# Weight decode, v rows, key low parts, mixed tokens and the transfer plan of an attention and channel-mix kernel

## The chip, the cores and the metric

The kernel runs on one core of a Trainium2 chip. A core has five engines that run their own instruction queues and wait for each other through semaphores: TensorE (PE in the profile), VectorE (DVE), ScalarE (ACT), GpSimd (POOL) and SyncE (SP). Here SP issues every DMA. The metric is device time in microseconds, lower is better. A measured time is the median of several executions, and a profile is of one execution.

## The reference

The program is an attention layer whose output feeds a channel mix with a gate:

```python
# q, k, v: (8, 8, 1152, 64)
q_pool = q.reshape(B, H, S // 2, 2, D).mean(axis=3)        # 576 pooled queries
scores = scale * np.matmul(q_pool, k.transpose(0, 1, 3, 2))
scores = scores - np.max(scores, axis=-1, keepdims=True)
attn = np.exp(scores)
attn = attn / (np.sum(attn, axis=-1, keepdims=True) + 1e-09)
out = np.matmul(attn, v)                                   # (8, 8, 576, 64) -> x: (8, 576, 512)
x_prev = np.concatenate([zeros, x[:, :-1, :]], axis=1)
xk = mu_k * x + (1.0 - mu_k) * x_prev
xr = mu_r * x + (1.0 - mu_r) * x_prev
k = np.maximum(xk @ w_k, 0.0)                              # w_k: 512 x 1024
v = k * k @ w_v                                            # w_v: 1024 x 512
r = 1.0 / (1.0 + np.exp(-(xr @ w_r)))                      # w_r: 512 x 512
return r * v
```

There are 64 heads (8 batches of 8), and 4,608 mixed tokens of 512 features.

## The kernel before, in words

**Precision.** All products run on 16-bit operands, with each fp32 operand split into a high and a low part; three products (high by high, high by low, low by high) then stand for one.

**Attention.** A head has 1,152 keys in 9 chunks of 128, and 576 queries in 6 blocks of 96. `prep` loads a head's k and v, casts k to fp16 (L397, ScalarE), subtracts for the low part (L399, VectorE), and transposes both by DMA in two pieces of 5 and 4 chunks (L404). v gets a high part (L412), a low part (L415) and a scaled copy `vb` (L418). The tile `vt` has rows of 130 fp16 elements per key chunk, `vb` rows of 66. `queries` does the same for the pooled queries of two heads. `block` multiplies a block's scores into one of three PSUM tiles `s` (L445), takes their maximum on VectorE (L452, L458) with two small matmuls (L455, L460), writes the negative maximum into the low query operand (L463), adds the low products (L469), and takes the exponential (L475). GpSimd makes the low part of the exponentials (L477). `window` multiplies 128 queries' exponentials with v: nine chunks of three matmuls (L495 and L497 from `vt`, L502 from `vb`) into the PSUM bank `a`; a head has five windows, all in that bank. The bank is then divided by the row sums (L517 to L520), and after every second head it is transposed (L532) and copied to the token tile `xt` (L535).

**Channel mix.** Tokens go in 18 tiles of 256. `mix` blends each token with the one before it, feature chunk by feature chunk: L604 on ScalarE, L607 on VectorE into the fp32 tile `xk` or `xr`. The matmul's high operand is the upper half of each fp32 word, read in place as bf16 with a step of two elements (`top`); L612 on VectorE subtracts it for the low part `xlk` or `xlr`. `ff` does, per tile, 96 products for `w_k` with 256 moving columns, and per 128 tokens 12 products for `w_r` and 24 for `w_v` with 512 moving columns, all on L632. The relu, the square and the gate run on ScalarE, VectorE and GpSimd.

**Weights.** The three weight tensors arrive as words in which `weights` finds a value in two pieces. They come in 20 chunks of 128 by 512, each loaded by L553 and rebuilt once: L564 on ScalarE writes to the PSUM bank `f`; L566, L567 and L569 on VectorE shift it and join sign and low bits; L571 casts to the high part and L572 on GpSimd subtracts for the low part. The bank `f` also holds the channel mix's products.

**Order.** Nothing is issued as the loops are written. Each piece of work is handed to a planner (`Issue`) with a duration, the buffers it reads and writes, and a key. The planner plays the whole program forward and backward twelve times against its own table of durations and latencies, keeps the shortest order that it finds, and the instructions are then issued in that order on each engine, DMAs too.

The first channel-mix tile needs all 8 heads of batch 0 and all of `w_k`. From then on PE has channel-mix products to put between the attention's blocks.

Of the kernel before, what the change touches and what calls it, by code (L numbers as in the profile page):

```python
# [3 lines left out]

# [42 lines left out]
LATE, SLACK = 0.08, 0.1  # L47


class Issue:  # L50

    LAT = {("DMA", "*"): 2.0, ("*", "DMA"): 1.22, ("PE", "DMA"): 1.46, ("PE", "PE"): 0.0,
           ("PE", "ACT"): 0.26, ("PE", "DVE"): 0.2, ("DVE", "PE"): 0.17, ("ACT", "PE"): 0.17,
           ("ACT", "POOL"): 0.18, ("DVE", "POOL"): 0.155, ("POOL", "PE"): 0.11, ("ACT", "DVE"): 0.142,
           ("DVE", "ACT"): 0.128, ("DVE", "DVE"): 0.12, ("ACT", "ACT"): 0.13, ("POOL", "POOL"): 0.13}  # L60

# [3 lines left out]
    def lat(self, a, b):  # L65
        for k in ((a, b), (a, "*"), ("*", b)):
            if k in self.LAT:
                return self.LAT[k]
        return 0.18

    def add(self, eng, dur, fn, r=(), w=(), key=0.0, port=None, tail=2.0):
# [23 lines left out]
        self.ops.append((eng, dur, fn, key, deps, eng == "POOL" if port is None else port, tail))  # L95

    @staticmethod
    def play(eng, dur, pred, succ, prio, wait, port):
# [3 lines left out]
        left = [len(p) for p in pred]
        ready = [0.0] * N
        start = [0.0] * N
        free, pend, avail = {}, {}, {}
        way = 0.0
        for n in range(N):
            e = eng[n]
            if e not in free:
                free[e], pend[e], avail[e] = 0.0, [], []  # L110
            if not left[n]:
                heapq.heappush(pend[e], (0.0, n))
        push, pop = heapq.heappush, heapq.heappop
        for _ in range(N):
# [17 lines left out]
            key, n = pop(av)  # L132
            if port[n] and way > t:

# [6 lines left out]
                else:  # L141
                    soon = [(rt, prio[m], m) for rt, m in pe if not port[m] and rt < way]
                    if soon:
                        rt, k2, m = min(soon)
                        push(av, (key, n))
                        pe.remove((rt, m))
                        heapq.heapify(pe)
# [620 lines left out]
```

## Time and profile before

| | us |
|---|---|
| median of 3 runs (1186.74 to 1193.13) | 1187.83 |
| span of the profiled execution, first to last instruction | 1190.5 |
| PE, DVE, ACT, POOL busy in the span | 1127.0, 933.5, 839.2, 527.8 |
| PE without a matmul in flight in the first 170 us | 55.1 |
| the same in all that follows | 8.4 |

The span is the profiled execution's own time as far as the profile gives it; nothing else is listed for that execution. It lies 2.7 us above the median of the timed runs and inside their range. A matmul's busy time in the profile is its time in flight (about 194 ns for 65 columns), and many are in flight at once, so PE's busy share tells when it has nothing to do, and the steps between the starts of its matmuls tell how fast it goes.

### The profile page before, as it was taken

Reading aid. Unit: us, or ns where it says so; the run is one execution under the profiler, and the core shown is the slowest. Engines: PE = TensorE matmul, PEld = TensorE weight load, DVE = VectorE, ACT = ScalarE, POOL = GpSimd, SP = SyncE. Lnnn points to the kernel's source line nnn. Section 1 sums busy time; section 2 is a strip of 40 time slices with the busy share of each in tenths; the row PEclk is TensorE's granted clock in tenths of the full one; section 3 lists DMA queues with packets and bytes.
Section 4 is the critical chain, followed back from the end, with each engine's and each line's share of the span. In section 5 each row is a group of like instructions: output and inputs, shape, how many; then the busy total and the mean of one; then the engine's idle time right before and its main releaser. Section 6 shows DMA issues by size and latency. Waiting matters only on the chain.

```text
span 1190.5 us, 45818 instructions
## 1 busy us (share of the span) xinstructions
PE 1127.0 (95%) x19504; PEld 933.0 (78%) x19504; DVE 933.5 (78%) x1827; ACT 839.2 (70%) x1674; POOL 527.8 (44%) x549
## 2 busy tenths in 40 slices
PE   3868689999999999999999999999999999999998
PEld 3757687888879787888888787979787888888565
DVE  5879898888798888888888878888887888774431
ACT  4767767777877777777878687776877777765543
POOL 2546455454545444544545354545354444533111
PEclk9989889999999999999999999999999999999999
DMA  8777754656555553545455544544455444210000
GB/s 199 176 164 167 174 113 112 131 122 136 101 110 138 125 115 74 114 119 110 100 117 116 120 104 102 115 95 110 107 113 110 100 86 100 51 35 2 28 18 27
DMA packets 226412, 126.71 MB, mean 106 GB/s; under 512 B 161696, under 2 KB 198560, under 8 KB 226208
## 3 DMA queue, kind: packets, MB, share of 16 engines
q1 hardware_dynamic: 226208, 123.79, 46.8%
q8 instruction: 152, 2.49, 0.9%
q14 instruction: 52, 0.43, 0.1%
HBM read 67.11 MB, written 9.44 MB: 64 GB/s over the span
## 4 chain that ended last, share of the span: by engine, by line
PE 85%; DVE 5%; ACT 4%; DMA 3%; issue 2%; SPq 0%; POOL 0%; ACTq 0%; DVEq 0%
PE f L632 33%; PE s L445 11%; PE s L469 11%; PE a L502 7%; PE a L495 7%; PE a L497 7%; PE s L632 4%; DVE mx L452 2%; ACT pf L475 2%; PE s L455 2%; PE a L632 2%; PE s L460 1%; PE a L532 1%; DMA qT<-qn 1%; DMA vr<-in_v_dram 1%
## 5 line engine op out<-in xcount | busy, mean ns | idle before, releaser
L477 POOL TENSOR_SCALAR pl<-pf 128x864 f16<-128x864 uint16 x384 | 379.1, 987 | 445.3 <-ACT pf L475 429.1
L452 DVE TENSOR_REDUCE mx<-s 128x96 f16<-128x864 f32 x384 | 402.8, 1053 | 83.5 <-PE s L445 47.2
L475 ACT ACTIVATE pf<-s 128x864 int32<-128x864 f32 x384 | 337.5, 890 | 103.2 <-PE s L469 81.6
L445 PE MATMUL s<-qT,ks 128*128 128x96 f16 x3456 | 222.4, 208 | 29.2 <-ACT pf L475 14.7
L497 PE MATMUL a<-vt,pf 128*128 128x64 f16 x2880 | 233.9, 194 | 0.0
L495 PE MATMUL a<-vt,pf 128*128 128x65 f16 x2880 | 233.5, 194 | 0.0
L469 PE MATMUL s<-qT,ks 128*128 128x96 f16 x3456 | 218.8, 209 | 14.6 <-ACT qT L463 11.3
L445 PEld LDWEIGHTS <-ks 128*128 128x128 f16 x3456 | 186.1, 99 | 52.6 <-issue 23.8
L469 PEld LDWEIGHTS <-ks 128*128 128x128 f16 x3456 | 184.3, 99 | 35.3 <-issue 13.5
L495 PEld LDWEIGHTS <-pf 128*128 128x128 f16 x2880 | 202.0, 99 | 6.7
L497 PEld LDWEIGHTS <-pf 128*128 128x128 f16 x2880 | 193.1, 98 | 8.2
L463 ACT ACTIVATE qT<-s 1x96 f16<-1x96 f32 x384 | 92.5, 243 | 104.3 <-PE s L460 94.1
L458 DVE TENSOR_REDUCE mb<-s 96x1 f16<-96x128 f32 x384 | 109.0, 285 | 71.5 <-PE s L455 65.0
L502 PE MATMUL a<-vb,pl 128*128 128x65 f16 x2880 | 153.9, 194 | 3.4 <-POOL pl L477 3.4
L632 PE MATMUL f<-xk,wk_lo 128*128 128x256 bf16 x496 | 136.9, 276 | 0.0
L632 PE MATMUL f<-xk,wk_hi 128*128 128x256 bf16 x496 | 136.8, 276 | 0.1
L632 PE MATMUL f<-xlk,wk_hi 128*128 128x256 f16 x496 | 134.4, 271 | 0.1
L502 PEld LDWEIGHTS <-pl 128*128 128x128 f16 x2880 | 122.8, 99 | 8.0 <-POOL pl L477 3.8
L663 POOL TENSOR_TENSOR gl<-g 128x512 f16<-128x512 f32 x72 | 78.5, 1091 | 104.6 <-ACT g L661 102.7
L632 PEld LDWEIGHTS <-wk_hi 128*128 128x128 f16 x1152 | 104.6, 97 | 13.0 <-issue 0.2
L632 PE MATMUL f<-wv_hi,g 128*128 128x512 f16 x240 | 90.9, 379 | 1.1 <-ACT em L682 1.1
L632 PE MATMUL f<-wv_hi,gl 128*128 128x512 f16 x240 | 90.9, 379 | 0.0
(90 smaller groups left out, 1895.0 us busy)
## 6 DMA issues: line engine op xcount, KB each, us to landing
kr<-in_k_dram SPq DMA_DIRECT2D x64, 288.0 KB, 3.2
vr<-in_v_dram SPq DMA_DIRECT2D x64, 288.0 KB, 3.3
qr<-in_q_dram SPq DMA_DIRECT2D x32, 320.0 KB, 3.7
ks<-ks SPq DMA_DIRECT2D x64, 144.0 KB, 3.1
out_dram<-em SPq DMA_DIRECT2D x36, 256.0 KB, 2.2
qr<-in_q_dram SPq DMA_DIRECT2D x32, 256.0 KB, 3.4
st<-in_moe_w_k_dram SPq DMA_DIRECT2D x8, 512.0 KB, 4.8
st<-in_moe_w_v_dram SPq DMA_DIRECT2D x8, 512.0 KB, 4.3
```

Of the source, the lines that this page charges most:

```text
L445: nc.tensor.matmul(cols(c, c + 1), ks1[hp][:, c, :], qhi, start=(c == c0), stop=False, skip_group_check=True)
L452: op("DVE", 0.967, lambda: nc.vector.tensor_reduce(mxz, grid(0, NC).rearrange("p c q -> p q c"), axis=AX.X, op=ALU.max), r=[("s", z)], w=[ ...
L458: op("DVE", 0.199, lambda: nc.vector.tensor_reduce(mbz[0:QN], s[0:QN, 0:P], axis=AX.X, op=ALU.max), r=[("s", z)], w=[("mb", z)], key=t + O ...
L463: op("ACT", 0.133, lambda: nc.scalar.activation(qlo[QN:QN + 1], s[QN:QN + 1, 0:QN], AF.Prelu, scale=1.0 - EPS, alpha=(1.0 + EPS) / (1.0 - ...
L469: nc.tensor.matmul(cols(c, c + 1), ks2[hp][:, c, :], qlo, start=False, stop=True, skip_group_check=True)
L475: op("ACT", NC * QN / 1200 + 0.051, lambda: nc.scalar.activation(pf[:, :, rows], grid(0, NC), AF.Exp, bias=SHIFT, scale=0.125 / (2.0 * SQ) ...
L477: op("POOL", NC * QN / 1000 + 0.066, lambda: nc.gpsimd.tensor_scalar(pl[:, :, rows], half(pf, U16, 0)[:, :, rows], LO, 1.0, op0=ALU.mult, ...
L495: nc.tensor.matmul(a_b[:, a0:a0 + VN], half(pf, F16, 1)[:, c, rows], vt[jv][:, c, D:D + VN], start=(w == 0 and c == 0), stop=False, skip_g ...
L497: nc.tensor.matmul(a_b[:, a0:a0 + D], half(pf, F16, 1)[:, c, rows], vt[jv][:, c, 0:D], start=False, stop=False, skip_group_check=True)
L502: nc.tensor.matmul(a_b[:, a0:a0 + VN], pl[:, c, rows], vb[jv][:, c, 0:VN], start=False, stop=(c == NC - 1), skip_group_check=True)
L632: nc.tensor.matmul(ps, terms[i][0], terms[i][1], start=(first and i == 0), stop=(i == last), skip_group_check=True)
L663: op("POOL", 2 * n * 0.0018 + 0.1, lambda f2=f2: nc.gpsimd.tensor_tensor(gl[:, f2, 0:n], g32[:, f2, 0:n], gh[:, f2, 0:n], op=ALU.subtract) ...
```

## The change

- The weights' low bits are converted by ScalarE (L587 of the changed kernel, into the buffer `em`), and the word is rebuilt in the SBUF buffer `ex` rather than in the PSUM bank `f`. VectorE has two steps per chunk (L590, L598) where it had three. Variants `"A"` and `"P"` of the code are not used (`DEC_K`, `DEC_RV` are `"D"`).
- Rows of `vt` have 136 elements and rows of `vb` 72, so each starts at a multiple of 16 bytes. The columns that are read are the same.
- For the first 8 heads GpSimd subtracts the key's low part instead of VectorE (`KN_POOL`), and windows of every second of these heads go to the bank `f` instead of `a` (`ALT`).
- A mixed token chunk is cast by ScalarE (L641) to its own contiguous fp16 tile `xh`, and this is the matmul operand in place of the strided upper halves. The fp32 chunk lies in one of three small buffers `xm`.
- A head's keys, and two heads' queries from the second pair on, are transposed by one DMA instead of two.
- The planner treats the DMAs as one line: a DMA has an issue time and a load, transfers land in order, and SP runs at most 8 us ahead of the line. The forward plan starts from keys with noise of a fixed seed. Several durations in its table are other numbers. A tile's two halves (`"k"` and `"r"`) are handed over by two calls of `ff`.

```diff
+KN_POOL, VT_POOL, XL_POOL = 8, 0, 0
+DEC_K, DEC_RV = "D", "D"
+ALT = 1
+QSPLIT = 1
+WDEP = [("ks1", 1), ("ks2", 0), ("vr", 1)]
+AHEAD2 = 0
+SEED, SPREAD = 2, 1.0
...
+    ISSUED, LANDED, AHEAD = 1.44, 0.52, 8.0
...
+            if e == "DMA" and ahead:
+                line = max(t + self.ISSUED, line) + load[n]
+                free[e] = max(end, line - self.AHEAD)
+                land = line + self.LANDED
+            elif e == "DMA":
+                free[e] = land = t + max(dur[n], load[n])
...
+        rnd = random.Random(SEED)
+        start, _ = self.play(p, succ, pred, [o[3] + rnd.gauss(0.0, SPREAD) for o in ops], wait, True)
...
-    vt = bufs("vt", NV, [P, NC, 2 * D + 2], F16)
-    vb = bufs("vb", NV, [P, NC, D + 2], F16)
+    vt = bufs("vt", NV, [P, NC, 2 * D + 8], F16)
+    vb = bufs("vb", NV, [P, NC, D + 8], F16)
...
-    xm = {n: const.tile([P, NG, T], F32, name=f"x{n}") for n in "kr"}
-    xl = {n: const.tile([P, NG, T], F16, name=f"xl{n}") for n in "kr"}
+    xm = bufs("xm", 3, [P, T], F32)
+    xl = {n: bufs(f"xl{n}", 1, [P, NG, T], F16) for n in "kr"}
+    xh = {n: bufs(f"xh{n}", 1, [P, NG, T], F16) for n in "kr"}
...
+        for j0, j1 in JS if n < QSPLIT else ((0, NQ),):
...
-            op("DVE", nn / 960 + 0.069, lambda cs=cs: nc.vector.tensor_tensor(
+            e, en, d = ("POOL", nc.gpsimd, nn * 0.0022 + 0.1) if n < KN_POOL else ("DVE", nc.vector, nn / 960 + 0.069)
+            op(e, d, lambda cs=cs, en=en: en.tensor_tensor(
                 kn[i][:, cs, D:P], kr[i][:, cs], kn[i][:, cs, 0:D], op=ALU.subtract),
                r=[("kr", i), ("kn", i, c0)], w=[("knl", i, c0)], key=key + 1, port=True)
-        for c0, c1 in ((0, 5), (5, NC)):
-            cs = slice(c0, c1)
-            op("DMA", 0.14 * (c1 - c0) + 0.08, lambda cs=cs: nc.sync.dma_start_transpose(
-                ks1[i][:, cs], kn[i][:, cs].rearrange("p c x -> p (c x)")),
-               r=[("kn", i, c0), ("knl", i, c0)], w=[("ks1", i, c0)], key=key + 1, tail=2.0)
+        op("DMA", 1.22, lambda: nc.sync.dma_start_transpose(ks1[i], kn[i].rearrange("p c x -> p (c x)")),
+           r=[(x, i, c) for x in ("kn", "knl") for c in (0, 5)], w=[("ks1", i)], key=key + 1, load=1.28)
...
+        bank, ka = (f_b, ("f",)) if ALT and n < H and n % 2 else (a_b, ("a",))
...
-                u, kf = f_b, ("f",)
-                ui = u.bitcast(I32)
-                op("ACT", 0.48, lambda u=u, wh=wh: nc.scalar.activation(u, wh.bitcast(F32), AF.Abs, scale=2.0 ** -111),
-                   r=[ks], w=[kf], key=key)
-                v_(0.6, lambda ui=ui: nc.vector.tensor_scalar(ui, ui, 3, None, op0=ALU.logical_shift_left), [kf], [kf])
-                v_(0.6, lambda ui=ui, wh=wh: nc.vector.scalar_tensor_tensor(
-                    ui, wh, -0x80000000, ui, op0=ALU.bitwise_and, op1=ALU.bitwise_or), [ks, kf], [kf])
-                v_(0.6, lambda ei=ei, ui=ui, wl=wl: nc.vector.scalar_tensor_tensor(
-                    ei, wl, 29, ui, op0=ALU.logical_shift_right, op1=ALU.bitwise_or), [ks, kf], [ke])
...
+                op("ACT", 0.48, lambda e=e, wh=wh: nc.scalar.activation(e, wh.bitcast(F32), AF.Abs, scale=2.0 ** -111),
+                   r=[ks], w=[ke], key=key)
...
+                    op("ACT", 0.48, lambda mi=mi, wl=wl: nc.scalar.activation(
+                        mi, wl.bitcast(U32), AF.Copy, scale=2.0 ** -29 * (1.0 - 2.0 ** -18), bias=-0.5 + 7.5 * 2.0 ** -18),
+                       r=[ks], w=[km], key=key)
+                    v_(0.6, lambda ei=ei, mi=mi: nc.vector.scalar_tensor_tensor(
+                        ei, ei, 3, mi, op0=ALU.logical_shift_left, op1=ALU.bitwise_or), [ke, km], [ke])
...
+                    v_(0.6, lambda ei=ei, wh=wh: nc.vector.scalar_tensor_tensor(
+                        ei, wh, -0x80000000, ei, op0=ALU.bitwise_and, op1=ALU.bitwise_or), [ks, ke], [ke])
...
-            op("DVE", n / 960 + 0.069, lambda c=c: nc.vector.tensor_tensor(
-                xl[w][:, c, 0:n], xm[w][:, c, 0:n], hi[:, c, 0:n], op=ALU.subtract),
-               r=[("x", w, c, False), ("x", w, c, True)], w=[("xl", w, c)], key=key + c * dk, port=True)
+            op("ACT", n / 1200 + 0.093, lambda c=c, x_m=x_m: nc.scalar.copy(xh[w][y][:, c, 0:n], x_m[:, 0:n]),
+               r=kx, w=[("xh", w, y, c)], key=key + c * dk)
...
+            op(e_, d, lambda c=c, x_m=x_m, en=en: en.tensor_tensor(
+                xl[w][y][:, c, 0:n], x_m[:, 0:n], xh[w][y][:, c, 0:n], op=ALU.subtract),
+               r=kx + [("xh", w, y, c)], w=[("xl", w, y, c)], key=key + c * dk, port=True)
```

How the orders stand to each other is shown at three places.

VectorE, the start of the weight decode, some 26 us into the program before. The names are those of the text above; the numbers behind them tell buffers apart. Before:

```order
L566 TENSOR_SCALAR f<-f 128x512
L452 TENSOR_REDUCE mx_94<-s_128 128x96
L458 TENSOR_REDUCE mb_96<-s_127 96x1
L567 SCALAR_TENSOR_TENSOR f<-st_120,f 128x512
L458 TENSOR_REDUCE mb_97<-s_128 96x1
L452 TENSOR_REDUCE mx_95<-s_129 128x96
L569 SCALAR_TENSOR_TENSOR ex_116<-st_120,f 128x512
L458 TENSOR_REDUCE mb_98<-s_129 96x1
L399 TENSOR_TENSOR kn_76<-kr_70,kn_76 128x5x64
```

With the change, at the first decoded chunk:

```order
L469 TENSOR_REDUCE mx_93<-s_132 128x96
L590 SCALAR_TENSOR_TENSOR ex_121<-ex_121,em_123 128x512
L475 TENSOR_REDUCE mb_96<-s_132 96x1
L598 SCALAR_TENSOR_TENSOR ex_121<-st_125,ex_121 128x512
L469 TENSOR_REDUCE mx_94<-s_133 128x96
L469 TENSOR_REDUCE mx_95<-s_134 128x96
L475 TENSOR_REDUCE mb_97<-s_133 96x1
```

A chunk has two steps instead of three, with both inputs in SBUF (`ex`, `em`, `st`) instead of one in PSUM (`f`), and the key's subtraction (L399) is gone from this queue.

SyncE's queue, from the first key transposes on. Before:

```order
L404 DMA_TRANSPOSE ks_0_79<-kn_76 128x5x128
L404 DMA_TRANSPOSE ks_0_79<-kn_76 128x4x128
L364 DMA qr_74<-in_q_dram 128x5x128
L380 DMA_TRANSPOSE qT_83<-qn_78 128x5x128
L404 DMA_TRANSPOSE ks_1_80<-kn_77 128x5x128
L380 DMA_TRANSPOSE qT_83<-qn_78 128x5x128
L407 DMA ks_0_81<-ks_0_79 64x1152
```

With the change:

```order
L421 DMA_TRANSPOSE ks_0_79<-kn_76 128x9x128
L408 DMA kr_70<-in_k_dram 128x576
L380 DMA qr_74<-in_q_dram 128x4x128
L380 DMA qr_74<-in_q_dram 128x5x128
L398 DMA_TRANSPOSE qT_83<-qn_78 128x4x128
L398 DMA_TRANSPOSE qT_83<-qn_78 128x5x128 x2
L423 DMA ks_0_81<-ks_0_79 64x1152
```

The keys of head 0 go in one transpose of 9 chunks. The queue has 444 rows where it had 569.

ScalarE in the middle of the program, where a token tile is mixed. Before:

```order
L604 ACTIVATE tmp_113<-xt_104,omu_r 128x128
L463 ACTIVATE qT_83<-s_128 1x96
L475 ACTIVATE pf<-s_128 128x9x96
L604 ACTIVATE tmp_113<-xt_104,omu_r 128x128
L463 ACTIVATE qT_83<-s_129 1x96
L397 CAST kn_76<-kr_70 128x5x64
```

With the change:

```order
L641 CAST xhk_110<-xm_107 128x256
L492 ACTIVATE pf<-s_132 128x9x96
L633 ACTIVATE tmp_118<-xt_104,omu_k 128x256
L633 ACTIVATE tmp_119<-xt_104,omu_k 128x256
L641 CAST xhk_110<-xm_105 128x256
L480 ACTIVATE qT_84<-s_133 1x96
```

The casts of mixed chunks (L641) stand between the exponentials (L492) and the maximum's writes (L480).

More of the change, by code (lines that the diff above doesn't have):

```diff
@@ L65, in lat, with add @@
     def lat(self, a, b):
[L66 to L71, printed above, removed]
+        if a == "DMA":
+            return 0.0
+        return self.LAT.get((a, b), 1.22 if b == "DMA" else 0.18)
+    def add(self, eng, dur, fn, r=(), w=(), key=0.0, port=None, load=0.0):
         n = len(self.ops)
@@ L94, in add, with play @@
                 self.rd.setdefault(b, []).append(n)
-        self.ops.append((eng, dur, fn, key, deps, eng == "POOL" if port is None else port, tail))
-    @staticmethod
-    def play(eng, dur, pred, succ, prio, wait, port):
+        self.ops.append((eng, dur, fn, key, deps, eng == "POOL" if port is None else port, None, (dur, load)))
+    def play(self, p, succ, pred, prio, wait, ahead):
+        eng, dur, port, load = p
         N = len(eng)
[L102 to L106, printed above, removed]
+        left = [len(x) for x in pred]
+        ready, start = [0.0] * N, [0.0] * N
+        free, pend, avail = ({e: v() for e in ("PE", "DVE", "ACT", "POOL", "DMA")} for v in (float, list, list))
+        push, pop = heapq.heappush, heapq.heappop
         for n in range(N):
-            e = eng[n]
-            if e not in free:
-                free[e], pend[e], avail[e] = 0.0, [], []
             if not left[n]:
-                heapq.heappush(pend[e], (0.0, n))
-        push, pop = heapq.heappush, heapq.heappop
+                push(pend[eng[n]], (0.0, n))
+        way = line = total = 0.0
         for _ in range(N):
@@ L141, in play @@
                 else:
-                    soon = [(rt, prio[m], m) for rt, m in pe if not port[m] and rt < way]
+                    soon = [x for x in pe if not port[x[1]] and x[0] < way]
                     if soon:
[L144 to L147, printed above, removed]
-                        key, n, t = k2, m, max(rt, t)
+                        rt, m = min(soon)
+                        instead(m, rt)
+                        key, n, t = prio[m], m, max(rt, t)
                     else:
@@ L172, in play, with follow @@
                     push(pend[eng[m]], (ready[m], m))
[L173 to L176 removed]
+        return start, total
+    def follow(self, p, succ, pred, order):
+        eng, dur, port, load = p
         N = len(eng)
[L180 to L181 removed]
+        ready, left, start = [0.0] * N, [len(x) for x in pred], [0.0] * N
         queue, at, free = {}, {}, {}
@@ L186, in follow @@
             at[e], free[e] = 0, 0.0
-        way, total = 0.0, 0.0
+        way = line = total = 0.0
         for _ in range(N):
```

251 lines of the change are left out of this document (142 added, 109 removed).

## The prediction

> **What bounds the kernel now.** I read the stretches of busy time first, because a share over the whole span mixes stages. Columns: stretch in us, its length, busy us of PE, PEld, DVE, ACT and POOL with their instructions, the granted clock, the DMA share.
>
> ```profile
> 0.00:170.00 170.00, 114.94 (x2217) 103.83 (x2218) 137.62 (x270) 109.28 (x215) 81.59 (x91) 0.90 0.75 167
> 13.00:170.00 157.00, 114.94 (x2217) 103.73 (x2217) 129.36 (x245) 103.68 (x203) 78.25 (x80) 0.89 0.73 164
> 160.00:170.00 10.00, 8.25 (x126) 7.42 (x126) 9.97 (x17) 7.01 (x17) 5.84 (x6) 0.83 0.50 121
> 170.00:180.00 10.00, 10.00 (x212) 9.47 (x209) 8.58 (x20) 7.62 (x15) 5.13 (x6) 1.00 0.78 124
> 200.00:1000.00 800.00, 796.18 (x14437) 667.00 (x14436) 674.74 (x1323) 603.42 (x1214) 372.89 (x384) 1.00 0.50 111
> 1090.00:1180.00 90.00, 90.00 (x609) 55.06 (x606) 33.01 (x69) 41.11 (x83) 14.83 (x14) 1.00 0.05 19
> ```
>
> There are two stages. From 170 us to the end PE never lacks work: 796.18 of 800 us, at a clock of 1.00. There only shorter matmuls save time. Before 170 us PE has nothing in flight for 55 us, and VectorE is the busiest, 129.36 of the 157 us after the first matmul (82%; ScalarE 66%). The waits of PE say the same. Columns: us in total, times, longest. The upper three rows are of 0 to 170 us, the last two of all that follows.
>
> ```profile
> PE s L445 <- DMA qT<-qn: 13.5, 2, 13.2
> PE s L445 <- ACT pf L475: 12.8, 20, 1.8
> PE s L469 <- ACT qT L463: 10.6, 10, 7.2
> ...
> PE s L445 <- ACT pf L475: 1.8, 5, 0.7
> PE s L469 <- ACT qT L463: 0.7, 2, 0.5
> ```
>
> 13.2 us is the wait for the first operands. The next two are one chain: maximum on VectorE, then ScalarE, then PE. This stage ends when PE gets channel-mix products, at 164 to 170 us. In both orders the first of these is nearly the same matmul of PE's queue, the 2,110th before and the 2,109th now, so PE's work ahead of it is the same, and an earlier start is worth its shift in full.
>
> **The change part by part. First stage.** The prices, with minimum, median and maximum in ns where three numbers stand, otherwise busy us and mean ns:
>
> ```profile
> L566 DVE TENSOR_SCALAR f<-f x20: 680/689/700, 25.2 to 161.6; 128x512 int32<-128x512 int32 x20
> L567 DVE SCALAR_TENSOR_TENSOR f<-st,f x20: 672/682/697, 27.0 to 162.3; 128x512 int32<-128x512 int32 x20
> L569 DVE SCALAR_TENSOR_TENSOR ex<-st,f x20: 669/674/689, 32.5 to 163.3; 128x512 int32<-128x512 int32 x20
> L687 DVE SCALAR_TENSOR_TENSOR ex<-ex,em x36: 651/683/1153, 201.3 to 1183.7; 128x512 f32<-128x512 f32 x36
> L612 DVE TENSOR_TENSOR xlk<-xk x72: 405/415/1256, 147.1 to 1148.1; 128x256 f16<-128x256 f32 x72
> ...
> L687 DVE SCALAR_TENSOR_TENSOR ex<-ex,em 128x512 f32<-128x512 f32 x36 | 26.2, 729 | 25.4 <-ACT em L685 25.3
> L612 DVE TENSOR_TENSOR xlk<-xk 128x256 f16<-128x256 f32 x72 | 39.0, 554 | 0.2
> L399 DVE TENSOR_TENSOR kn<-kr,kn 128x320 f16<-128x320 f32 (+1 forms) x128 | 64.2, 512 | 0.2 <-ACT kn L397 0.2
> L564 ACT ACTIVATE f<-st 128x512 f32<-128x512 f32 x20 | 12.7, 636 | 3.3 <-DVE ex L569 2.3 <-DMA st<-in_moe_w_k_dram 0.9
> L572 POOL TENSOR_TENSOR wk_lo<-ex,wk_hi 128x512 f16<-128x512 f32 x8 | 9.5, 1182 | 10.2 <-DVE f L566 8.1 <-ACT wk_hi L571 1.8
> L397 ACT CAST kn<-kr 128x256 f16<-128x256 f32 x64 | 25.9, 404 | 2.3 <-DMA ks<-kn 1.8
> L571 ACT CAST wk_hi<-ex 128x512 f16<-128x512 f32 x8 | 4.9, 615 | 0.1
> ```
>
> VectorE up to the fourth low part of the first tile, by the rows of its queue: 20 chunks with three steps before, now 16 first and 15 second steps. That takes away 20 x 0.689 + 5 x 0.682 + 4 x 0.674 = 19.9 us. Sixteen subtractions go to GpSimd: 16 x 0.512 = 8.2 us. One more maximum and three small steps stand there now: about 2.6 us.
>
> The two steps that stay read two SBUF inputs, while L567 and L569 read one from PSUM. Their spreads are 25 and 20 ns. L687 with both inputs in SBUF has a median of 683 but single ones to 1153, and a mean of 729; L612 has a mean of 554 against a median of 415. So a two-input step costs 46 to 139 ns more on average; I take 100, for 31 steps 3 us. The Trainium skill ("SBUF — State Buffer", section "SBUF: two separate sides") gives a reason: a VectorE operation with two SBUF inputs and a GpSimd operation take a shared port pair as an exclusive lock, and the later one blocks. By that rule alone, with GpSimd busy 82 of 170 us and its operations about 1 us, each of the 31 steps would wait 0.24 us on average, 7.4 us in all instead of 3; the spreads agree with it in kind.
>
> VectorE: 137.6 - 19.9 - 8.2 + 2.6 + 3 = 115 us. ScalarE gains a conversion per chunk: by its 51st exponential 17 x 0.636 = 10.8 us, loses 3 x 0.636 + 4 x 0.615 = 4.4 us as three Abs and four casts come later, and gets five casts of mixed chunks (5 x 0.404) and two blends, 3 us: 109.3 + 9.4 = 118.7 us. So ScalarE becomes the busier engine. Behind its conversion stand exponentials, for which PE and GpSimd wait. GpSimd gets 16 subtractions of 0.74 us (1.182 scaled to 320 elements; an estimate between 0.59 and 1.18), 12 us on 82, far from a bound.
>
> From 13 us on VectorE has 107 us and ScalarE 113. If the busier engine reaches the 82% that VectorE reaches now, the stage lasts 113 / 0.82 = 138 us and ends at 151 instead of 170. If VectorE still rules, 107 / 0.82 = 130, end at 143. If two engines in turn lame each other, nothing is gained. At the start head 0's key went through these two subtractions:
>
> ```profile
> 4.79 0.48 DVE L399 TENSOR_TENSOR kn<-kr,kn 128x320 f16<-128x320 f32 x1
> ...
> 5.59 0.42 DVE L399 TENSOR_TENSOR kn<-kr,kn 128x256 f16<-128x256 f32 x1
> ```
>
> On GpSimd they take about 1.3 us instead of 0.9, and the first scores wait for them; I add 1 us with the longer transpose. I take **18 us**, bounds 0 and 26.
>
> The DMAs hardly decide this. Their share is 0.75 and the bytes are the same; over 151 us the share would be 0.84, less four weight loads that now come later. One transpose per key saves SP issue time:
>
> ```profile
> 10.70 1.23 SPq L404 DMA_TRANSPOSE ks<-kn  x1
> ks<-kn SPq DMA_TRANSPOSE x128, 2.6
> ```
>
> An issue takes 1.23 us and lands 2.6 us after it; nine chunks at once cost between one and two issues, so 0 to 1.2 us per head is saved on SP. The whole key comes later than its first piece did, at most by one issue, but a head ahead of its use, behind six blocks of the head before it; without that cover it would be 1.2 us per head. The second bank lets odd heads of batch 0 start while the other bank is divided and copied. All of it is at nothing, inside the bounds above.
>
> **Rows of v.** In PE's timeline (start, us in flight from first to last, count) nine matmuls follow each other like this:
>
> ```profile
> 603.72 0.45 PE L502 MATMUL a<-vb,pl 128*128 128x65 f16 x9
> 604.01 0.19 PE L495 MATMUL a<-vt,pf 128*128 128x65 f16 x1
> ...
> 306.45 0.19 PE L495 MATMUL a<-vt,pf 128*128 128x65 f16 x1
> ...
> 307.00 0.28 PE L632 MATMUL f<-xk,wk_hi 128*128 128x256 bf16 x1
> ...
> L502 PE MATMUL a<-vb,pl 128*128 128x65 f16 x2880 | 153.9, 194 | 3.4 <-POOL pl L477 3.4
> ```
>
> L502: (604.01 - 603.72) / 9 = 32 ns per step. The 18 of L495 and L497 from 306.45 to 307.00 take 30.6. Between 250 and 1080 us I sorted the starts of L502 by key chunk: chunks 0, 4 and 8 take 29.2 to 29.5 ns, all others 32.3 to 34.4, mean 31.7. A `vb` row is 132 bytes, so just these three rows start at a multiple of 16 bytes. That is the strongest evidence in the trace for this edit: now every row does, and I give each 29.2. Saved: 2.5 ns x 2,880. For `vt` the mean of a pair is 60.1 and the pattern is less clean (28.3 to 31.5, the high steps in different places for the two); I take 2 x 29.2 = 58.4, so 1.7 x 2,880. Seven of eight heads lie in PE's stage: (7.2 + 4.9) x 7/8 = **10.6 us**, bounds 0 and 13 (pairs down to 29.2 + 28.3).
>
> **Contiguous tokens.** 24 products of `w_k` run from 307.00 above to this row:
>
> ```profile
> 309.69 0.32 PE L502 MATMUL a<-vb,pl 128*128 128x65 f16 x5
> ...
> 307.11 0.27 PE L632 MATMUL f<-xlk,wk_hi 128*128 128x256 f16 x1
> 307.22 0.28 PE L632 MATMUL f<-xk,wk_lo 128*128 128x256 bf16 x1
> ...
> 1147.31 0.38 PE L632 MATMUL a<-wv_hi,g 128*128 128x512 f16 x1
> ...
> 1150.34 0.38 PE L632 MATMUL a<-wv_hi,gl 128*128 128x512 f16 x1
> ```
>
> 2.69 us / 24 = 112.1 ns. Over 250 to 1080 us the step of a strided `xk` is 114.4 and that of the contiguous `xlk` 108.6. The 512-column products, contiguous, take 3.03 / 14 = 216.4, half of it 108.2. So 1,152 strided products save 5.8 ns: **6.7 us**, all in PE's stage; the lower bound is 0, if the type (bf16) and not the stride costs nothing to change. `w_r` and `w_v` have the strided operand stationary and stay at 216.
>
> The price is 144 casts on ScalarE, 404 ns each by the row of the same form: 58 us. The 139 casts behind the first stage are 56 us in some 1,020, so 44 in 800, where ScalarE has 603: 647 of some 783, or 83%, with VectorE at 86%. Both stay below PE, whose own time hides the casts. PE's idle time there is 3.8 us in 800; with less slack on both I add **3 us** for the whole stage. Without that cover all 56 us would count.
>
> **Sum**, against the profiled execution: 1190.5 - 18 - 10.6 - 6.7 + 3 = 1158.2. The median lies 2.7 below its span: **1155 us**.
>
> **The rivals.**
>
> *ScalarE takes over the first stage.* For it: it had 66% against VectorE's 82% and gets 9 us while VectorE loses 22, and it sits between PE and GpSimd. Against it: 113 us are still fewer than VectorE's 129. No gain there: 1173.
>
> *The steps do not shorten.* The long steps may come from something that stays: the turn of weight loads and PSUM columns that goes along with the chunk, or the high product itself. For it: the steps of L495 and L497 do not follow the rows' starts as those of L502 do. Against it: 114.4 beside 108.6 for equal shapes, and the three aligned chunks. Then 17.3 us fall away: 1172. The Trainium skill ("SBUF — State Buffer", section "Specifications (TRN2)") points this way: reads keep full bandwidth with two or more hits per 16-byte line, and a step of two bf16 still has four, so by that rule the stride was free; the 114.4 does not agree with it.
>
> *Slower: the casts pass through to PE.* They stand between the exponentials and the writes of L463, which PE waits for, in a queue in order. If each of the 139 casts behind the first stage delays PE by its 404 ns: 1155 - 3 + 56 = 1208. It decides from 36 us on, when two of three casts go straight through. Against it: in all the time after 170 us PE waits 1.8 + 0.7 us for these two, and has channel-mix products to run meanwhile.
>
> *The order gives it back.* The new plan rests on other prices and noise. PE's idle time after 170 us is 8 us; a plan that leaves 40 ends at 1187, no change.
>
> **How the numbers follow.** Forecast 0.62, ScalarE in the first stage 0.13, no shorter steps 0.11, slower 0.08, given back 0.06. The forecast's own bounds: all at best 1190.5 - 26 - 13 - 6.9 - 2.7 = 1142, and 1167 with a third of the first stage's gain lost (6) and a third of the steps' (6). The range takes in the second and third case at 1173 and 1172, and a little below 1142 for a better plan: 1138 to 1176. About 0.5% can be told from no change in this kernel (1182 to 1194). Faster: 0.62 + 0.13 + 0.11 = 0.86; same 0.06; slower 0.08.
>
> **What would show it.** PE's first channel-mix product at 146 to 152 us and the clock at 1.00 from there on; ScalarE ahead of VectorE before it; nine steps of the `vb` product in 0.26 us; 24 products of `w_k` in 2.60 us; PE's idle time after that below 12 us; maxima above 900 ns in the two decode steps. It is wrong if the first product still comes after 165 us, if nine `vb` steps still take 0.29 us, or if PE waits for the exponentials in the middle of the program.

## The result, and the profile after

The changed kernel takes **1163.35 us** (median of 4 runs, 1163.05 to 1164.27), beside 1190.48 of the kernel before in the same comparison (1186.74 to 1193.46). The ratio is 0.9775, with a 95% interval of 0.9752 to 0.9798: about 27 us less. The forecast was 1155, with a range of 1138 to 1176.

The profiled execution of the changed kernel took 1164.27 us and its span is 1162.5, so 1.8 us lie around the span. Its page begins like this (busy us, share of the span, instructions):

```profile
PE 1111.6 (96%) x19504; PEld 926.0 (80%) x19504; DVE 908.2 (78%) x1791; ACT 888.7 (76%) x1838; POOL 550.0 (47%) x565
```

ScalarE is up by 50 us and VectorE down by 25. The stretches of busy time, with the columns of the prediction, first of the kernel before, then of the changed one:

```profile
0.00:180.00 180.00, 124.94 (x2426) 113.30 (x2426) 146.20 (x289) 116.90 (x230) 86.72 (x97) 0.91 0.75 165
180.00:1190.50 1010.50, 1002.06 (x17083) 819.68 (x17080) 787.26 (x1538) 722.29 (x1445) 441.10 (x453) 1.00 0.43 96
```

```profile
13.00:143.00 130.00, 101.46 (x2120) 91.46 (x2120) 112.17 (x201) 105.36 (x207) 87.63 (x85) 0.97 0.76 181
0.00:180.00 180.00, 136.37 (x2724) 121.50 (x2725) 149.41 (x278) 143.42 (x282) 115.13 (x120) 0.98 0.72 171
180.00:1162.50 982.50, 975.26 (x16783) 804.52 (x16781) 758.75 (x1515) 745.24 (x1557) 434.91 (x445) 1.00 0.44 98
200.00:1000.00 800.00, 797.33 (x14672) 678.06 (x14671) 664.96 (x1331) 635.04 (x1328) 383.33 (x394) 1.00 0.51 112
```

In the first 180 us PE starts 2,724 matmuls where it started 2,426, has nothing in flight for 43.6 us instead of 55.1, and is granted a clock of 0.98 instead of 0.91. After that it is as full as before: 982.5 - 975.3 = 7.2 us without a matmul in flight, against 8.4. The first channel-mix product comes at 143 us instead of 164; the row gives start, length and operation:

```profile
143.07 0.27 PE L665 MATMUL f<-xhk,wk_hi 128*128 128x256 f16 x1 [0.83 <-ACT xt L553]
```

PE's largest waits in the changed kernel, over the whole span (us in total, times, longest), are the first operands and the same two as before:

```profile
PE s L462 <- DMA qT<-qn: 15.1, 1, 15.1
PE s L462 <- ACT pf L492: 13.0, 28, 1.4
PE s L486 <- ACT qT L480: 6.7, 13, 2.6
```

### The profile page after: what moved, and what is told of

Read it like the earlier page. It is cut to its first block, busy times and chain, and to the rows that moved or that the text cites. A ratio compares the mean times of both kernels' runs of the same rounds, so it can differ in the third digit from the quotient of the medians.

```text
span 1162.5 us, 45688 instructions
## 1 busy us (share of the span) xinstructions
PE 1111.6 (96%) x19504; PEld 926.0 (80%) x19504; DVE 908.2 (78%) x1791; ACT 888.7 (76%) x1838; POOL 550.0 (47%) x565
## 4 chain that ended last, share of the span: by engine, by line
PE 85%; ACT 6%; DVE 3%; DMA 2%; issue 2%; POOL 1%; SPq 0%; DVEq 0%; ACTq 0%
PE f L665 33%; PE s L462 11%; PE s L486 11%; PE a L520 6%; PE a L515 6%; PE a L513 6%; PE s L665 4%; ACT pf L492 2%; PE s L472 2%; PE a L665 2%; DVE mx L469 1%; PE s L477 1%; PE a L550 1%; DMA st<-in_moe_w_k_dram 1%; ACT qT L480 1%
## 5 line engine op out<-in xcount | busy, mean ns | idle before, releaser
L494 POOL TENSOR_SCALAR pl<-pf 128x864 f16<-128x864 uint16 x384 | 385.0, 1003 | 405.4 <-ACT pf L492 378.3
L492 ACT ACTIVATE pf<-s 128x864 int32<-128x864 f32 x384 | 337.4, 890 | 70.5 <-PE s L486 45.8
L462 PE MATMUL s<-qT,ks 128*128 128x96 f16 x3456 | 221.2, 207 | 28.6 <-DMA qT<-qn 15.1
L462 PEld LDWEIGHTS <-ks 128*128 128x128 f16 x3456 | 185.5, 99 | 54.6 <-issue 22.9
L515 PE MATMUL a<-vt,pf 128*128 128x64 f16 x2700 | 227.6, 194 | 0.0
L513 PE MATMUL a<-vt,pf 128*128 128x65 f16 x2700 | 227.2, 193 | 0.0
L486 PE MATMUL s<-qT,ks 128*128 128x96 f16 x3456 | 214.5, 207 | 7.2 <-ACT qT L480 6.7
L513 PEld LDWEIGHTS <-pf 128*128 128x128 f16 x2880 | 204.1, 99 | 6.0 <-ACT pf L492 0.4
L486 PEld LDWEIGHTS <-ks 128*128 128x128 f16 x3456 | 180.9, 98 | 28.5 <-issue 7.7
L515 PEld LDWEIGHTS <-pf 128*128 128x128 f16 x2880 | 194.8, 98 | 7.8 <-issue 0.3
L480 ACT ACTIVATE qT<-s 1x96 f16<-1x96 f32 x384 | 91.9, 243 | 99.8 <-PE s L477 87.6
L475 DVE TENSOR_REDUCE mb<-s 96x1 f16<-96x128 f32 x384 | 108.6, 285 | 57.9 <-PE s L472 53.3
L520 PE MATMUL a<-vb,pl 128*128 128x65 f16 x2700 | 143.4, 193 | 0.5 <-POOL pl L494 0.5
L665 PE MATMUL f<-xhk,wk_hi 128*128 128x256 f16 x496 | 135.1, 272 | 1.3 <-ACT xt L553 0.8
L665 PE MATMUL f<-xhk,wk_lo 128*128 128x256 f16 x496 | 135.1, 272 | 0.0
L472 PE MATMUL s<-identb,mx 128*96 128x128 f16 x384 | 87.1, 227 | 4.9 <-DVE mx L469 4.5
```

The source lines that it names most:

```text
L462: nc.tensor.matmul(cols(c, c + 1), ks1[hp][:, c, :], qhi, start=(c == c0), stop=False, skip_group_check=True)
L472: op("PE", 0.057, lambda: nc.tensor.matmul(s[0:QN, 0:P], mxz, identb, start=False, stop=False, skip_group_check=True), r=[("mx", z)], w=[( ...
L475: op("DVE", 0.199, lambda: nc.vector.tensor_reduce(mbz[0:QN], s[0:QN, 0:P], axis=AX.X, op=ALU.max), r=[("s", z)], w=[("mb", z)], key=t + O ...
L480: op("ACT", 0.133, lambda: nc.scalar.activation(qlo[QN:QN + 1], s[QN:QN + 1, 0:QN], AF.Prelu, scale=1.0 - EPS, alpha=(1.0 + EPS) / (1.0 - ...
L486: nc.tensor.matmul(cols(c, c + 1), ks2[hp][:, c, :], qlo, start=False, stop=True, skip_group_check=True)
L492: op("ACT", NC * QN / 1200 + 0.051, lambda: nc.scalar.activation(pf[:, :, rows], grid(0, NC), AF.Exp, bias=SHIFT, scale=0.125 / (2.0 * SQ) ...
```

## The experiments

Each run is compared with the kernel before on the same chip. That kernel's medians were 1190.9, 1190.8 and 1189.9 in the three groups of runs. The differences to the changed kernel are between groups, so one of 1 or 2 us is weak.

Counts of matmuls tell little of the work done, since one of 64 columns takes 30 ns and one of 512 columns 216. The last column therefore weighs every matmul that started in the profile's first 180 us with the step that its form takes at a clock of 1.00 (30 ns for 64 and 65 columns, 42 for 96, 56 for 128, 109 for 256 and for the fp32 transposes, 216 for 512). It is an estimate from the traces; the whole program has 1,076 us of such work.

| kernel | us, median (lowest to highest) | to the changed kernel | PE's work started by 180 us, us |
|---|---|---|---|
| kernel before | 1190.48 (1186.74 to 1193.46) | +27.1 | 93 |
| changed kernel | 1163.35 (1163.05 to 1164.27) | | 112 |
| before_rows | 1187.85 (1185.58 to 1191.85) | +24.5 | 94 |
| rows_undone | 1165.16 (1163.97 to 1165.22) | +1.8 | 112 |
| tokens_strided | 1168.31 (1167.61 to 1168.84) | +5.0 | 114 |
| rows_64_bytes | 1162.62 (1162.16 to 1162.79) | -0.7 | 113 |
| first_stage_undone | 1170.46 (1167.11 to 1172.03) | +7.1 | 106 |
| old_decode | 1170.78 (1169.82 to 1170.97) | +7.4 | 107 |
| key_low_on_vector | 1174.20 (1172.82 to 1176.54) | +10.9 | 104 |
| seed_3 | 1181.39 (1181.05 to 1183.31) | +18.0 | 102 |
| no_noise | 1175.13 (1173.64 to 1177.01) | +11.8 | 108 |
| old_plan | 1181.69 (1179.33 to 1183.83) | +18.3 | 100 |
| old_decode_seed_48 | 1165.03 (1163.55 to 1165.35) | +1.7 | 113 |
| combined | 1159.11 (1157.48 to 1162.50) | -4.2 | 114 |

### PE's steps, with every engine's order kept

**The rows of v undone.**

```diff
-    vt = bufs("vt", NV, [P, NC, 2 * D + 8], F16)
-    vb = bufs("vb", NV, [P, NC, D + 8], F16)
+    vt = bufs("vt", NV, [P, NC, 2 * D + 2], F16)
+    vb = bufs("vb", NV, [P, NC, D + 2], F16)
```

> The changed kernel with v rows of 130 and vb rows of 66 elements again, everything else and every engine's order the same. Forecast's theory (a row that starts off a 16-byte boundary costs, and costs again in every step): the time rises by about 10 us, to 1173. Rival (the start is only one of two costs; the other, 28 against 35 ns steps, stays with aligned rows, as the profile after shows): the vb step goes from 30.4 back to 31.7 ns, the vt pair stays near 60, and the time rises by 3 to 5 us. If rows don't matter: within 1 us of 1163.4.

Measured: 1.8 us more; the ranges of the two kernels' runs just overlap. A run of nine `vb` products in PE's timeline (start, us in flight from first to last, count), first of the changed kernel, then of this one:

```profile
402.16 0.44 PE L520 MATMUL a<-vb,pl 128*128 128x65 f16 x9
```

```profile
402.31 0.45 PE L520 MATMUL a<-vb,pl 128*128 128x65 f16 x9
```

One is hardly shorter than the other. The steps between starts, sorted by key chunk over 200 to 1050 us (some 2,300 of each kind, mean ns for chunks 0 to 8), show why:

```
rows of 130 and 66 (rows_undone)
  vt, 65 columns (L513)  29.4 29.2 31.0 31.0 29.2 29.4 30.5 31.2 29.2   mean 30.0
  vt, 64 columns (L515)  31.3 30.7 28.4 29.7 30.2 31.6 29.4 28.4 31.0   mean 30.1
  vb, 65 columns (L520)  29.5 34.5 32.5 32.4 29.2 32.1 33.1 32.7 29.1   mean 31.7
rows of 136 and 72 (changed kernel)
  vt, 65 columns (L513)  29.6 29.2 29.2 29.4 29.2 29.2 29.4 29.2 29.3   mean 29.3
  vt, 64 columns (L515)  31.7 30.2 30.9 32.2 30.0 31.3 32.1 30.1 31.4   mean 31.1
  vb, 65 columns (L520)  29.4 33.0 29.5 30.2 29.6 30.3 32.4 29.5 29.9   mean 30.4
```

The rows' starts do cost: with aligned rows every L513 step is 29.3 ns. But the step behind it (L515) takes back more than was won there, 31.1 for 30.1, and two chunks of `vb` stay at 32 to 33. Single L515 steps are either 27 to 29 or 33 to 35 ns. So the pair has gained nothing (60.4 for 60.1) and `vb` 1.25 ns: (1.25 - 0.35) x 2,520 = 2.3 us, beside the 1.8 measured.

**Only the rows, in the kernel before.**

```diff
-    vt = bufs("vt", NV, [P, NC, 2 * D + 2], F16)
-    vb = bufs("vb", NV, [P, NC, D + 2], F16)
+    vt = bufs("vt", NV, [P, NC, 2 * D + 8], F16)
+    vb = bufs("vb", NV, [P, NC, D + 8], F16)
```

> The kernel before with only the row lengths changed (136 and 72 elements), same orders. Forecast's theory: 10.6 us less than before. Rival (only the vb step gains, about 1.3 ns of 2,880): 3 to 5 us less. Neither: within 1 us of the kernel before on the same chip.

Measured: a ratio of 0.9979 (0.9961 to 0.9996), so 0.5 to 4.6 us less, 2.5 in the middle. Its steps are 29.3, 31.1 and 30.4, as in the changed kernel. The 10.6 us of the forecast are excluded by both runs.

**Rows at multiples of 64 bytes.**

```diff
-    vt = bufs("vt", NV, [P, NC, 2 * D + 8], F16)
-    vb = bufs("vb", NV, [P, NC, D + 8], F16)
+    vt = bufs("vt", NV, [P, NC, 2 * D + 32], F16)
+    vb = bufs("vb", NV, [P, NC, D + 32], F16)
```

> The changed kernel with rows of 160 and 96 elements, so that rows start at multiples of 64 bytes. Same orders. If the steps of 33 to 35 ns that stay come from a coarser alignment of the moving rows, the vb step falls from 30.4 to about 29.3 and the vt pair from 60.4 to about 58: 8 us less, 1155. If they come from something else (the weight loads, other readers), steps and time stay as they are, 1163.

Measured: 0.7 us less, and steps of 29.3, 31.1 and 30.4 ns, the same. A coarser alignment of the moving rows isn't what the long steps lack. What makes them long stays open: they change from one pass to the next in the same window, chunk and buffer (L515 in the fifth window's fifth chunk: 35, 28, 35, 35, 29, 28 ns in six heads whose v lies in the same buffer), so it is no fixed address alone.

**Mixed tokens strided again, as fp16.**

```diff
-    xh = {n: bufs(f"xh{n}", 1, [P, NG, T], F16) for n in "kr"}
+    xh = {n: [t_[:, :, :, 1] for t_ in bufs(f"xh{n}", 1, [P, NG, T, 2], F16)] for n in "kr"}
```

> The changed kernel with the cast mixed chunks written to every second fp16 element, so that the matmul reads them with a step of two again, but as fp16. Same orders. Theory (the stride costs): the step of the high products rises from 109.7 to about 114.4 ns, 1,152 of them, plus 5 us. Rival (the bf16 type cost it): steps stay at 109.7 and the time within 1 us of 1163.4.

Measured: 5.0 us more. 24 products of `w_k` in the chain of work that ended last (start, us, count), of the changed kernel and of this one:

```profile
288.10 2.62 PE f L665 x24
```

```profile
286.84 2.69 PE f L665 x24
```

2.69 us is what they took in the kernel before. The steps are 114.2 and 114.7 ns for the two strided products, with fp16 as with bf16, and 109.2 contiguous. The strided write also makes each cast on ScalarE longer, 484 ns instead of 406 in the median; it isn't what costs the 5 us, as PE's idle time after 180 us is 7.3 us, against 7.2. The stride of the moving operand costs it, not the type.

### The first stage, with a new plan each

**All engine edits of the first stage undone.** Old decode through the bank `f`, all key subtractions on VectorE, one bank. The plan's model of the transfers and the single transposes stay.

```diff
-KN_POOL, VT_POOL, XL_POOL = 8, 0, 0
+KN_POOL, VT_POOL, XL_POOL = 0, 0, 0
-ALT = 1
+ALT = 0
...
+                u, kf = f_b, ("f",)
+                v_(0.6, lambda ui=ui: nc.vector.tensor_scalar(ui, ui, 3, None, op0=ALU.logical_shift_left), [kf], [kf], port=None)
...
```

> The changed kernel with the old decode (three VectorE steps through the bank f, no conversion on ScalarE), all key subtractions on VectorE and one bank for all windows; new plan, single transposes, v rows and mixed tokens stay. The order is planned anew. Forecast's theory (the busier of VectorE and ScalarE sets the end of the first stage): VectorE has 22 us more, the first channel-mix product comes at about 168 us instead of 151 and the time is 1163 + 18 = 1181. Rival (the plan of the transfers and the single transposes gave the 20 us): the product stays near 151 to 154 and the time near 1165.

Measured: 7.1 us more, between the two theories. The first channel-mix product comes at 151.5 us, where the rival had it, and not at 168. The stretches:

```profile
13.00:150.00 137.00, 108.10 (x2118) 97.59 (x2118) 125.03 (x238) 98.96 (x198) 73.29 (x76) 0.89 0.80 186
0.00:180.00 180.00, 136.66 (x2685) 124.54 (x2686) 157.05 (x310) 128.50 (x258) 93.11 (x104) 0.91 0.74 171
```

With the old amount of VectorE work, VectorE is at 125 of 137 us, 91%, where the old plan had held it at 81%. PE has started 106 us of work by 180 us: 13 of the 19 us that the change had gained, without the engine edits. And PE waits no longer than in the changed kernel: it has nothing in flight for 43.3 us of the 180, against 43.6. What differs is the granted clock, 0.91 against 0.98.

**Only the old decode.** The same edit of `weights` with `ALT = 0`; key subtractions stay on GpSimd for 8 heads.

> The changed kernel with only the old decode (and so one bank); key subtractions of the first heads stay on GpSimd. VectorE has 14 us more, ScalarE 11 us less. Forecast's theory: the first stage ends 13 to 16 us later, 1177. Rival (plan): 1165. If ScalarE was the bound in the changed kernel: no change or faster.

Measured: 7.4 us more, between the two again. The first channel-mix product comes at 159.8 us, 16.7 later than in the changed kernel, but with 273 more of the attention's matmuls ahead of it. So the time of that product measures the stage only where the work ahead of it is the same.

**Only the key subtractions back on VectorE.**

```diff
-KN_POOL, VT_POOL, XL_POOL = 8, 0, 0
+KN_POOL, VT_POOL, XL_POOL = 0, 0, 0
```

> The changed kernel with all key subtractions on VectorE. VectorE has 8 us more in the first stage, GpSimd 12 us less. If VectorE sets the end of the first stage (85% busy there): 1163 + 8 / 0.85 = 1173. If ScalarE does, as the forecast had it: within 3 us of 1163.

Measured: 10.9 us more, which is the number for VectorE as the bound. But undoing this edit and the decode together cost less (7.1), so the runs don't add up as two engine loads would.

**Another seed.** The control for all three:

```diff
-SEED, SPREAD = 2, 1.0
+SEED, SPREAD = 3, 1.0
```

> The changed kernel with another seed of the plan's noise, nothing else: what a new plan alone moves. If plans are alike, within 2 us of 1163; if the seed was picked out of many, 3 to 8 us slower. Differences of other runs with a new plan are read against this one.

Measured: **18.0 us more**, for the same instructions with the same operands in another order, more than any engine edit that was undone. Neither of the two expectations went as far.

```profile
0.00:180.00 180.00, 127.66 (x2522) 113.42 (x2523) 137.12 (x259) 135.58 (x267) 109.57 (x116) 0.95 0.65 163
180.00:1181.50 1001.50, 988.00 (x16984) 813.78 (x16983) 780.86 (x1533) 758.48 (x1572) 439.15 (x450) 1.00 0.43 97
```

PE starts 202 matmuls fewer by 180 us than in the changed kernel, and has 13.5 us without one in flight after that instead of 7.2. So one plan of each of two kernels says little of an edit: what the three runs above say of single edits is inside the scatter. This ended the theory of the engine loads and made the plan the suspect.

**The plan without its noise,** as the kernel before had it:

```diff
-SEED, SPREAD = 2, 1.0
+SEED, SPREAD = 2, 0.0
```

> The changed kernel with the plan's noise at zero, as the kernel before had it. It separates what the drawn noise gave from what the edits gave. If the 18 us that another seed cost was that seed's bad luck: within 3 us of 1163. If the seed of the change is the lucky one and the edits alone are worth less: 1170 to 1180, with the loss in the first 180 us and in the idle time after it.

Measured: 11.8 us more; of the three orders of these instructions, the one of the change is the lucky one.

```profile
0.00:180.00 180.00, 132.61 (x2683) 117.34 (x2684) 146.84 (x272) 142.48 (x279) 114.76 (x120) 0.98 0.70 170
180.00:1172.50 992.50, 982.12 (x16823) 808.22 (x16821) 775.36 (x1520) 749.16 (x1560) 430.81 (x445) 1.00 0.43 97
```

**The old planner, all other edits in place.** `Issue` of the kernel before, a DMA again an issue time and a fixed time to landing, with the old numbers:

```diff
-class Issue:
+class Issue:
+    OLD = {(0.45, 0.01): (0.46, 2.0), (1.22, 1.28): (1.34, 2.0), (1.22, 0.64): (0.71, 2.0), (0.42, 1.21): (0.36, 2.8),
+           (0.54, 0.9): (0.47, 2.5), (0.43, 2.41): (0.36, 4.5), (0.36, 0.3): (0.36, 2.0)}
```

> The changed kernel with the old planner (a DMA is an issue time and a fixed time to landing, the old table for the DMAs, no noise); all edits to the work stay, single transposes too. Theory now (the plan packs the first stage): the first stage loses more, as before, and the time is 1175 to 1185. Forecast's theory (the load of VectorE and ScalarE sets the end of the stage, whatever the plan): 1163 to 1168.

Measured: 18.3 us more, 8.2 less than the kernel before. The two edits of PE's steps account for 5.0 + 1.8 = 6.8 of the 8.2. That leaves 1.4 us for all edits to the first stage under the old planner, loosely: the 8.2 has an interval of 5.5 to 10.9, and it is one plan of each.

```profile
13.00:150.00 137.00, 101.67 (x2085) 91.69 (x2086) 111.23 (x195) 103.38 (x201) 83.02 (x84) 0.96 0.67 172
0.00:180.00 180.00, 128.56 (x2512) 116.20 (x2513) 143.91 (x262) 136.46 (x268) 106.05 (x115) 0.95 0.64 164
```

VectorE is busy 111 of 137 us, 81%, as long as in the kernel before, whose row for the same stretch is this:

```profile
13.00:150.00 137.00, 98.63 (x1913) 88.80 (x1913) 111.10 (x213) 90.77 (x177) 68.51 (x70) 0.89 0.78 172
```

PE has started 100 us of work by 180 us, 7 more than in the kernel before, where the changed kernel has started 19 more. Its first channel-mix product comes at 158.7 us.

**The old decode with a picked seed.** The kernel of old_decode, planned with the seed that came out shortest by the plan's own account:

```diff
-SEED, SPREAD = 2, 1.0
+SEED, SPREAD = 48, 1.0
```

> The kernel of old_decode (three VectorE steps through the bank f, one bank for the windows) with another seed, the one that comes out shortest by the plan's own account among many. If the new decode is worth VectorE's 14 us, it stays at 1170 or above. If the decode is worth little and the plan's luck makes the difference between old_decode and the changed kernel: 1161 to 1166.

Measured: 1165.0, 5.8 us below old_decode and 1.7 above the changed kernel. With a picked plan, the old decode and the single bank are as good within 2 us. No such run was made with the key subtractions back on VectorE.

```profile
0.00:180.00 180.00, 138.98 (x2714) 121.89 (x2715) 153.95 (x302) 133.67 (x269) 108.16 (x122) 0.97 0.71 175
180.00:1163.30 983.30, 975.92 (x16794) 805.14 (x16791) 763.08 (x1509) 742.43 (x1550) 432.74 (x444) 1.00 0.43 97
```

**A combination.** On the kernel of old_decode:

```diff
-KN_POOL, VT_POOL, XL_POOL = 8, 0, 0
+KN_POOL, VT_POOL, XL_POOL = 24, 0, 1200
-QSPLIT = 1
+QSPLIT = 64
-SEED, SPREAD = 2, 1.0
+SEED, SPREAD = 71, 1.0
...
+    vt = bufs("vt", NV, [P, NC, 2 * D + 32], F16)
+    vb = bufs("vb", NV, [P, NC, D + 32], F16)
```

The expectation speaks of one transpose for each pair's queries; in fact `QSPLIT = 64` splits the queries of every pair into two pieces.

> A version meant to beat both: the old decode and one bank, key subtractions of 24 heads and low parts of the first 1,200 tokens on GpSimd, all queries transposed by one DMA, rows of 64 bytes, and a seed picked by the plan's own account. If GpSimd's free half carries VectorE's work and the plan is what counts: 1156 to 1162. If two-input work on GpSimd holds up VectorE's (the shared port): 1165 or more.

Measured: **1159.1 us**, ratio 0.9745 (0.9719 to 0.9772) to the kernel before, 4.2 us below the changed kernel. PE starts 2,833 matmuls by 180 us:

```profile
0.00:180.00 180.00, 142.69 (x2833) 128.09 (x2834) 156.09 (x299) 138.74 (x281) 125.74 (x147) 0.95 0.79 183
180.00:1158.60 978.60, 972.59 (x16674) 800.66 (x16672) 736.66 (x1441) 738.14 (x1538) 464.20 (x491) 1.00 0.43 96
```

Its slowest run, 1162.50, lies just below the changed kernel's fastest, on another chip. Which of its parts gives this was not taken apart.

## Why the prediction was right or wrong

**Two stages, the first one idle on PE: right, with a term missing.** Some 20 of the 27 us lie in the first stage; after 180 us PE's steps are shorter and its idle time is 7.2 us for 8.4. An earlier start was worth its shift in full, because the work ahead was the same: in both traces the first channel-mix product is PE's 2,121st matmul (the prediction counted 2,110 and 2,109). But waiting was only two thirds of that shift. The 2,120 matmuls ahead took 164.0 us before, 55.0 without a matmul in flight and 109.0 with, at a granted clock of 0.90; they take 143.05 now, 41.6 without and 101.5 with, at 0.98. So 13.4 us are less waiting and 7.5 are time in flight. The prediction printed the 0.90 and had no term for it. In the kernel before, the clock is 0.50 between 163 and 165.4 us and 1.00 behind that, and the same product takes twice the step, 0.21 us and then 0.11:

```profile
164.22 0.41 PE L632 MATMUL f<-xlk,wk_hi 128*128 128x256 f16 x1
164.43 0.42 PE L632 MATMUL f<-xk,wk_lo 128*128 128x256 bf16 x1
...
165.53 0.27 PE L632 MATMUL f<-xlk,wk_hi 128*128 128x256 f16 x1
165.64 0.28 PE L632 MATMUL f<-xk,wk_lo 128*128 128x256 bf16 x1
```

What lowers the clock wasn't tested. It isn't the sum of the waiting alone: first_stage_undone waits 42.3 us ahead of its first product, as the changed kernel does, and is granted 0.90 there.

**The first stage, 18 us: the size came out by luck, the reason was wrong.** Of the 27.1 us, the two edits of PE's steps take 6.8 when undone singly; the remaining 20.3 are the first stage and a little less idle time behind it. The step that failed is "if the busier engine reaches the 82% that VectorE reaches now". VectorE's share is not a property of its work but of the order: the old plan with the lighter load keeps it at 81% and the stage stays long (old_plan), the new plan with the old load drives it to 91% (first_stage_undone). What the lighter load is worth alone is known loosely: 1.4 us under the old planner, 7.1 under the new one with the change's seed, and for the decode and the bank 1.7 between two picked plans. The order of the same instructions moves as much as the stage gained. From the old planner to the change's plan it is 18.3 us: 6.6 to the new planner without noise, 11.8 more from the drawn seed, and another seed gives 18.0 back. The 6.6 is from one plan each, and seeds scatter by more. So 18 met 20.3 by luck: the forecast put it on the engines' load, and with seed 3 the same loads would have left some 2 us of it.

Why a plan packs better isn't settled. No single wait of PE carries the difference in the first 180 us: old_plan has 3.1 us more than the changed kernel on ScalarE's writes of the maximum, 2.1 more on VectorE's `mb` and 1.3 more on the exponentials; seed_3 has 3.8 more on the exponentials, 3.4 more on `mb` and 3.5 on a copy of the keys. That the model of the transfers is the reason, and not only the number of plans tried, wasn't tested with several seeds of each planner.

**ScalarE as the busier engine: wrong.** Up to the first product VectorE has 112 us from 13 on and ScalarE 105; the forecast had 107 and 113. The forecast's loads run to 170 us, six behind the first product of before, and ScalarE was busy for 3.9 of these six. Its 17 conversions took 11.5 us where 10.8 was taken (674 ns each, not 636), with 49 exponentials ahead and not 51. VectorE's load is larger although the forecast counted too far for it as well; one part is the low part of v, whose 15 steps (L431) took 646 ns in the mean there, where they had taken 493 (L415).

**Two SBUF inputs: right in kind and size.** The two decode steps, minimum, median and maximum in ns, and the table's means, with the key subtraction on GpSimd:

```profile
L590 DVE SCALAR_TENSOR_TENSOR ex<-ex,em x20: 674/682/1650, 30.4 to 170.6; 128x512 int32<-128x512 int32 x20
L598 DVE SCALAR_TENSOR_TENSOR ex<-st,ex x20: 673/680/1187, 31.2 to 178.8; 128x512 int32<-128x512 int32 x20
```

```profile
L590 DVE SCALAR_TENSOR_TENSOR ex<-ex,em 128x512 int32<-128x512 int32 x20 | 16.0, 802 | 1.1 <-ACT ex L580 1.1
L598 DVE SCALAR_TENSOR_TENSOR ex<-st,ex 128x512 int32<-128x512 int32 x20 | 14.4, 720 | 0.0
L587 ACT ACTIVATE em<-st 128x512 int32<-128x512 uint32 x20 | 13.5, 675 | 0.4 <-DMA st<-in_moe_w_k_dram 0.4
L418 POOL TENSOR_TENSOR kn<-kr,kn 128x320 f16<-128x320 f32 (+1 forms) x16 | 13.8, 878 | 5.4 <-ACT kn L415 4.9
```

The means lie 120 and 40 ns above the medians, 80 on average where 100 was taken. Five of the 40 steps make up all of it (949, 1150, 1187, 1639 and 1650 ns), so the average rests on few. Each of the five overlaps a GpSimd instruction; the 15 steps beside an idle GpSimd take 674 to 693 ns, and 20 overlap one and stay below 700. In the kernel before, 51 of the 60 steps with an input in PSUM overlap one, and none takes more than 700. By the lock rule of the Trainium skill ("SBUF — State Buffer", section "SBUF: two separate sides"), the estimate for random meetings was 240 ns a step. The five long steps agree with its blocking in kind, the 80 ns do not with that estimate. GpSimd's subtraction takes 878 ns, not 740, within the bounds.

**The rows of v, 10.6 us: mis-sized; 1.8 when undone, 2.5 when done alone.** The three aligned chunks of `vb` were read as the speed of every aligned row. Nine `vb` steps take 0.27 us, between the 0.26 forecast and the 0.29 of before. The experiments show a second cost in these steps that alignment doesn't touch, and that is larger in the step behind one that got shorter (L515, 31.1 ns for 30.1). For `vt` the trace of before had said so: its pattern was called "less clean", and 4.3 us were put on it nevertheless.

**Contiguous tokens, 6.7 us: right;** 5.0 when undone. The high products went from 114.4 to 109.2 ns, not to 108.6, and `xlk` from 108.6 to 109.1: 1,152 x 5.2 - 576 x 0.5 = 5.7 us by the steps. The rule of the Trainium skill ("SBUF — State Buffer", section "Specifications (TRN2)"), by which such a stride is free, does not agree with this: 114.4 ns against 109.2.

**The casts, +3 us: not there.** PE's idle time behind 180 us is 7.2 us, against 8.4, with ScalarE at 79% of the middle 800 us instead of 75%. A cast takes 406 and 404 ns in the median, as priced.

**The start, and the transposes.** The first scores begin at 15.1 us, 1.9 later than before (1 was taken). A whole key's transpose takes SP 1.30 us of issue, about what a piece took:

```profile
L421 SPq DMA_TRANSPOSE ks<-kn x64: 1243/1302/2234, 6.7 to 1026.7; - x64
ks<-kn SPq DMA_TRANSPOSE x64, 3.3
```

It lands after 3.3 us instead of 2.6. That is near the lower of the two prices, one issue and not two.

**From span to median, -2.7 us: not there.** The prediction took the median to lie 2.7 us below the profiled span, from three runs of the kernel before. A fourth run moves that kernel's median to 1190.48, its span; the changed kernel's median lies 0.9 above its span. So this term was off by 3.6 us, beside the 8.8 of the rows; the casts and the first stage came out better than forecast and hid part of it.

**The rivals.** "The order gives it back" had the right cause and the wrong place: it expected PE's idle time after 170 us to grow to 40. The order gave the stage's gain, and another order of the same kernel takes most of it away again (1181.4), 8.7 us of it as waiting in the first 180 us and 6.3 behind them. The casts passing through to PE, and ScalarE taking over, did not happen. That the steps don't shorten held for the `vt` pair and not for the tokens.

## What to carry to other kernels

Where a planner writes the order, give an edit's worth only against the scatter of plans: here one seed moved the time by 18 us, more than any single edit undone, and with a seed picked for the old decode the difference was 1.7 us where it had been 7.4. A busy share in a stage that is bound by chains of waits isn't a limit that a new load can be divided by; ask first whether another order would raise it, and read the granted clock of the stage beside the waits. A fast subset of steps in a trace proves that a cost exists, but the gain is to be taken from the mean over whole sequences, since a shortened step can hand its time to the next.
